# Attention followed by a two-layer MLP: one moe item moved in two units, one x multiply moved ahead of two norms, 14 more dummy matmuls

## The chip, the cores and the metric

The kernel runs on one core of one Trainium2 chip. The core has five engines that each work through their own queue in the order written: TensorE (PE, matmuls; PEld is its weight load), VectorE (DVE), ScalarE (ACT), GpSimd (POOL) and SyncE (SP, which here only issues DMAs). They meet through semaphores. The metric is the device time of one execution in microseconds (us). The profile is of one execution; its span, 415.2 us, runs from the first to the last instruction.

## The reference

```python
def rmsnorm(x, g):
    rms = np.sqrt(np.mean(x * x, axis=-1, keepdims=True) + 1e-06)
    return x / rms * g
q_n, k_n = rmsnorm(q, g_q), rmsnorm(k, g_k)        # (8, 12, 448, 64)
scores = np.matmul(q_n, k_n.transpose(0, 1, 3, 2)) / np.sqrt(64)
scores = scores - np.max(scores, axis=-1, keepdims=True)
attn = np.exp(scores)
attn = attn / (np.sum(attn, axis=-1, keepdims=True) + 1e-09)
x = np.matmul(attn, v)                             # heads side by side: (3584, 768)
h = x @ w_in                                       # w_in (768, 2048)
out = np.maximum(0.01 * h, h) @ w_out              # w_out (2048, 768)
```

## The kernel before, in words

Attention is cut into 24 units; unit u holds four heads of one batch, so three units make a batch, whose 448 positions then go through the MLP (called moe in the code). A unit has these stages, each a small function:

- Preparation, some units ahead: `load` fetches q and k, `load_v` v; `prep_sq`/`prep_sqp` square them (ACT or GpSimd), `prep_ssq` (L159, DVE) sums the squares, `prep_rinv` (L164, L165, ACT) makes the inverse root, `prep_norm` (L171, DVE) writes the normed q and k in fp16 as `n`. They are then transposed to `qkT`: on TensorE for the first units (L179 in `prep_tr`, with copies L753 and L755 on DVE), from unit 6 on by a DMA (`prep_trd`, L183), after which DVE multiplies the q part by the weights g (`prep_g`, L155).
- Scores: seven tiles of 64 keys for the four heads, in four steps d of one, two, two and two tiles (`STEPS`). `qk` (L199, TensorE) writes a tile into one of two score slots `sT` in PSUM; `ex` (L218, ACT) reads it, writes the exponential to `et` and thereby frees the slot.
- The shift inside the exponential: the maximum of the first tile (`shift_max`, L236, L238 on DVE, which makes `dg`), spread by a small matmul (`shift_mm`, L254 or L248) and read back as the bias `eb` (L255 or L249, L257).
- Sums and values: sums of `et` by matmuls with ones (L280, or L307 in `zcol`), `add_e` adds some tiles on DVE first (L292); the product with v is L367. The inverse of the sums is taken on ACT (L353, L354 in the first units; L327, L332 later, and then four DMAs, L337, spread it over the partitions as `rz`). The x multiply joins the two: `xmul` (L376), or L347 on DVE (`xmul_sb`) or on GpSimd (`xmul_pool`). It writes `xt`, the MLP's input.

The MLP of a batch is cut into items in a `queue`. A first-layer item (`moe1`, L389) is six matmuls of 128 x 448, over the six blocks of 128 inputs, into one PSUM bank `hps`, and an ACT prelu (L383) to `gt`. A second-layer item (L430) is eight matmuls of 128 x 384. The last two of the six matmuls of `moe1` read the part of `xt` that the third unit of the batch wrote.

All of the order is written by hand (`tc.manual_schedule`). The first three units are written out line by line; from unit 3 on a loop goes over units and steps. In step d it issues the scores, the exponentials and, in step 0, the sums, values and shift of the unit before. Then it gathers `jobs` (preparation of later units, x multiplies, weight differences L446 for the second layer) and calls `fill`, which takes items from the queue and issues one job after each item, and the rest of the jobs behind the last. How many items a step takes came from `fill` itself: it shared the cost of what is queued over the steps that are left before the next batch's items arrive, by the weights `WD`.

PSUM banks outside the score slots come from four buffers called `aux`, given out in turn; who gets a buffer waits until its last user is done. `warm` (L769) issues dummy matmuls of 128 x 128 whose result nobody reads; they keep TensorE busy in gaps. In the part of unit 2 the aux buffers are taken in this order: `pb` of unit 2 (shift), two for the value product of unit 1, one for the transposed q of unit 3, one for the transposed k of unit 3.

Of the kernel before, what the change touches and what calls it, by code (L numbers as in the profile page):

```python
# [18 lines left out]
def kernel(  # L19
# [18 lines left out]
    NU = B * NQ  # L38
# [73 lines left out]
    st = {}  # L112
# [62 lines left out]
    def prep_tr(u, ti, copies):  # L175
        tp = aux([P, NS, P], FP16, "tp")
        for (lo, hi), copy in copies:
            for x in range(lo, hi):
                nc.tensor.transpose(tp[:, x, :], buf(u, "n16")[:, ti, x].rearrange("p a d -> p (a d)"), ident16)  # L179
            copy(buf(u, "qkT")[:, ti, lo:hi], tp[:, lo:hi], ti == 0)  # L180
# [21 lines left out]
    def qk(u, steps):  # L202
        st[u]["sT"] = []
        for t in steps:
            sT = slot()
            score(u, t, (sT[:, 0], sT[:, 1]))
            st[u]["sT"].append((t, sT))

    def ex(u):
        s = st[u]  # L210
        if "et" not in s:
            s["et"] = epool.tile([P, NS, 2, S], FP16, tag="et", name="et")
        for t, sT in s["sT"]:
            if isinstance(sT, list):
                for a in range(2):
                    nc.scalar.activation(s["et"][:, t, a], sT[a][:, 0:S], AF.Exp, bias=s["eb"], scale=1.0)
            else:
                nc.scalar.activation(s["et"][:, t], sT[:, :, 0:S], AF.Exp, bias=s["eb"], scale=1.0)  # L218
# [6 lines left out]
    def shift_max(u):  # L225
        s = st[u]
        sT = s["sT"][0][1]
        if isinstance(sT, list):
            pm2 = small.tile([P, 2], FP32, tag="pm2", name="pm2")
            for a in range(2):  # L230
                nc.vector.tensor_reduce(pm2[:, a:a + 1], sT[a][:, 0:S], axis=AXL.X, op=ALU.max)
            s["spare"] = sT[0]
            nc.vector.tensor_reduce(s["spare"][:, 511:512], pm2, axis=AXL.X, op=ALU.max)
        else:
            s["spare"] = sT[:, 0]
            nc.vector.tensor_reduce(s["spare"][:, 511:512], sT[:, :, 0:S], axis=AXL.XY, op=ALU.max)  # L236
        s["dg"] = small.tile([P, P], FP16, tag="dg", name="dg")
        nc.vector.tensor_tensor(s["dg"], ident16, s["spare"][:, 511:512].broadcast_to([P, P]), op=ALU.mult)  # L238
# [131 lines left out]
    def xmul(u, rs=BOTH):  # L370
        s = st[u]
        b, g = divmod(u, NQ)
        if b not in xts:
            xts[b] = xpool.tile([P, NQ, 2, S], FP16, tag="xt", name="xt")
        for r in rs:
            nc.vector.tensor_tensor(xts[b][:, g, r], s["pv"][r][:, 0:S], s["rz"][:, r], op=ALU.mult)  # L376
            drop(s["pv"][r])
# [37 lines left out]
    def flush():  # L415
        while pend:
            pend.pop(0)()
# [247 lines left out]
    queue = []  # L665
# [50 lines left out]
            items += [(1.31, fn) for fn in std]  # L716
        queue.extend(items)

    WD = (3.6, 2.9, 2.8, 2.8)
    STEPS = ((0,), (1, 2), (3, 4), (5, 6))  # L720
    debt = [0.0]

    def narrow(u):
        return 4 <= u < NU - 1
# [1 line left out]
    def fed(u, d):  # L726
        return u % NQ == 0 and d == 3

    def fill(u, d, jobs):
        total = sum(c for c, _ in queue)  # L730
        left = WD[d] + 3.0
        uu, dd = u, d
        while True:
            dd += 1
            if dd == 4:
                uu, dd = uu + 1, 0
            if uu == NU or (fed(uu, dd) and (u > 3 or uu > 3)):
                break
            left += WD[dd]
        debt[0] += total * WD[d] / left  # L740
        while queue and debt[0] >= queue[0][0] * 0.5:
            c, fn = queue.pop(0)
            fn()
            debt[0] -= c
            if jobs:
                jobs.pop(0)()
        flush()
        for job in jobs:
            job()
# [17 lines left out]
    def warm(n, bank):  # L767
        for x in range(n):
            nc.tensor.matmul(bank[:, P:2 * P], onesp, onesp, start=True, stop=True)  # L769

    with tc.manual_schedule():
# [57 lines left out]
        def trn(u, ti, copy):  # L829
            prep_tr(u, ti, ((ALL, copy),))  # L830
# [91 lines left out]
        load_v(5)  # L922
        qk(2, (2,))
        ex(2)
        warm(6, st[2]["pb"])
        qk(2, (3,))
        ex(2)
        trn(3, 0, vcopy)
        trn(3, 1, vcopy)
        xmul(1)  # L930
        prep_ssq(4)
# [30 lines left out]
        for u in range(3, NU):  # L962
            for d in range(4):
                if d > 0 or u > 3:
                    qk(u, STEPS[d])
                    if d == 0:
                        shift_max(u)
                        if u == 6:
                            xmul_sb(u - 2)
                        if narrow(u - 1):  # L970
                            pv_slot(u - 1)
                            zcol(u - 1)
                            shift_mm(u)
                            pv_out(u - 1)
                        else:
                            zsum_slot(u - 1)
                            pv(u - 1)
                            shift_mm(u)
                            zinv(u - 1)
                    ex(u)  # L980
                    if d == 0 and narrow(u - 1):
                        zcol_ln(u - 1)
                if d == 2 and ADDED.get(u, 0) > 3 and u < NU - 1:
                    add_e(u)
                    if u > 4:
                        xmul_sb(u - 1)
                jobs = []

                def job(fn, *args):
                    jobs.append(lambda: fn(*args))  # L990

                if d == 0:
                    if u == 3:
                        prep_norm(4)
                        gate(4)
                    elif narrow(u - 1):
                        if u < NU - 1:
                            job(zcol_inv, u - 1)
                    else:
                        xmul(u - 1)  # L1000
                    if u + 4 < NU:
                        job(load, u + 4)
                    if u + 3 < NU:
                        load_v(u + 3)
                    if u < 6:
                        prep_sqp(u + 3)
                if d == 1 and narrow(u - 1) and not 5 <= u < 8 and ADDED.get(u, 0) < 4:
                    xmul_pool(u - 1)
                if u == NU - 1:
                    if d == 1:  # L1010
                        job(zcol_inv, u - 1)
                if fed(u, d) and u > 3:
                    push(u // NQ - 1)
                if (u, d) in ((3, 1), (4, 0)):
                    for ti in range(2):
                        prep_tr(u + 1, ti, VV)
                if d == 1 and 5 <= u < NU - 1:
                    job(prep_g, u + 1)
                if u + 2 < NU:
                    if d == 1:  # L1020
                        if ADDED.get(u) == 3:
                            job(lambda u: (prep_ssq(u + 2), add_e(u)), u)
                        else:
                            for ti in range(2):
                                job(prep_ssq, u + 2, ALL, (ti,))
                    if d == 2:
                        job(prep_rinv, u + 2)
                        for ti in range(2):
                            job(prep_norm, u + 2, ALL, (ti,))
                        if u > 3:  # L1030
                            job(prep_trd, u + 2)
                if d == 1 and 4 <= u < 8:
                    job(weight_sum, u - 4, 0)
                if d == 0 and 5 <= u < 9:
                    job(weight_sum, u - 5, 1)
                if d == 2 and u == 6:
                    job(xmul_sb, u - 1)
                if d == 1 and u == NU - 2:
                    jobs.append(lambda: None)
                    job(add_e, u)  # L1040
                if u == NU - 2 and d == 0:
                    for n, tile_ in ((1, (raws, "rq", 3)), (2, (raws, "rk", 3)), (3, None), (4, (prep_p, "sq", 3))):
                        job(win_sum, n, 1, tile_)
                    for n in (3, 1, 2, 4):
                        job(x_sum, LATE, n)
                if u == NU - 1 and d == 3:
                    job(add_e, u)
                    job(xmul_sb, u - 1)
                if d == 3 and 6 <= u < NU - 3:
                    for ti in range(2):  # L1050
                        job(prep_sq, u + 3, ALL, (ti,))
                fill(u, d, jobs)
# [4 lines left out]
        for i, ns in enumerate(((3, 1), (2, 4))):  # L1057
            c, fn = queue[i]
# [33 lines left out]
```

## Time and profile before

The median of three runs is 417.51 us (416.79 to 417.85).

| Stretch (us) | What | PE busy | DVE busy | ACT busy | PE clock | DMA share |
|---|---|---|---|---|---|---|
| 26.0 to 34.0 | end of unit 1, start of unit 2 | 6.35 of 8.0 | 6.88 | 7.32 | 1.00 | 1.10 |
| 34.0 to 42.4 | unit 2 | 7.35 of 8.4 | 7.56 | 7.37 | 1.00 | 1.12 |
| 42.4 to 57.7 | unit 3 | 14.41 of 15.3 | 12.78 | 13.46 | 1.00 | 1.15 |
| 57.7 to 70.8 | unit 4 | 12.55 of 13.1 | 11.67 | 10.19 | 1.00 | 0.95 |
| 70.8 to 84.5 | unit 5 | 13.60 of 13.7 | 12.25 | 7.68 | 1.00 | 0.99 |
| 84.5 to 97.8 | unit 6 | 13.08 of 13.3 | 11.41 | 10.01 | 1.00 | 1.00 |
| 97.8 to 112.0 | unit 7 | 14.20 of 14.2 | 12.48 | 12.99 | 1.00 | 0.66 |

A stretch is cut at the start of a unit's first exponential, roughly; busy times are unions of the engine's instructions inside it. The clock is the share that TensorE was granted. The DMA share is the time that packets took over the time of 16 engines; it can pass 1 because a packet that starts inside a stretch is counted whole. In the timeline, "[0.37 <-ACT et L218]" behind an instruction says how long its engine was idle before it, and which instruction ended that.

### The profile page before, as it was taken

The numbers are of one execution on the slowest core, as the hardware profiler recorded it, in microseconds if no ns is written. First come the engines' busy times: TensorE is split into PE (matmuls) and PEld (weight loads), VectorE is DVE, ScalarE is ACT, GpSimd is POOL, SyncE is SP. The second block draws the span as 40 slices with busy tenths as digits, with TensorE's granted clock in tenths as the row PEclk, the third lists the DMA queues.
The fourth block names the chain that finished last, engine by engine and source line by source line (L and its number), as shares of the span: only waits on it lengthen the run. The fifth ranks groups of instructions, "written<-read, shape, count | busy, mean of one in ns | idle before, by whom it ended". The sixth has DMA issues, their size and how long they took to land.

```text
span 415.2 us, 9343 instructions
## 1 busy us (share of the span) xinstructions
PE 399.3 (96%) x3817; PEld 219.1 (53%) x3817; DVE 307.7 (74%) x492; ACT 300.7 (72%) x470; POOL 68.4 (16%) x70
## 2 busy tenths in 40 slices
PE   8688999999999999999999999999999999999995
PEld 7444444554445544554445544454445557558863
DVE  5888898898788757867669757767669788557762
ACT  5898887677987699867987679867986657653600
POOL 1868432200020200010020200020001202000000
PEclk9999999999999999999999999999999999999999
DMA  6999999999565986678664896678552460032023
GB/s 207 259 255 253 240 249 141 229 174 207 138 154 92 224 213 125 150 173 182 155 155 72 220 196 136 170 147 185 158 103 47 120 160 8 10 75 77 2 55 98
DMA packets 71950, 62.41 MB, mean 150 GB/s; under 512 B 36324, under 2 KB 67044, under 8 KB 71908
## 3 DMA queue, kind: packets, MB, share of 16 engines
q1 hardware_dynamic: 61312, 49.62, 47.3%
q0 software_dynamic: 10272, 11.80, 18.3%
q8 instruction: 30, 0.49, 0.5%
q10 hardware_dynamic: 324, 0.39, 0.3%
q14 instruction: 12, 0.10, 0.1%
HBM read 45.61 MB, written 11.01 MB: 136 GB/s over the span
## 4 chain that ended last, share of the span: by engine, by line
PE 82%; DVE 9%; ACT 6%; issue 2%; DVEq 0%
PE hps L389 27%; PE sT L199 8%; PE sT L367 5%; PE ma L471 5%; PE op L430 5%; PE md L471 5%; PE bank L591 4%; PE mc L471 4%; PE bank L471 4%; ACT et L218 3%; PE mb L471 3%; PE zc L307 2%; DVE n L171 2%; PE warm L769 2%; PE sT L471 2%
## 5 line engine op out<-in xcount | busy, mean ns | idle before, releaser
L218 ACT ACTIVATE et<-sT,eb 128x896 f16<-128x896 f32 x166 | 159.4, 1008 | 26.7 <-PE sT L199 17.4
L389 PE MATMUL hps<-xt,win 128*128 128x448 f16 x600 | 121.0, 353 | 0.3 <-DVE xt L376 0.2
L389 PEld LDWEIGHTS <-win 128*128 128x128 f16 x612 | 56.8, 98 | 58.4 <-issue 10.0
L383 ACT ACTIVATE gt<-hps 128x448 f16<-128x448 f32 x100 | 53.9, 554 | 7.4 <-PE hps L389 6.4
L199 PE MATMUL sT<-qkT 64*64 64x448 f16 x664 | 52.5, 363 | 4.2 <-ACT et L218 2.8
L159 DVE TENSOR_REDUCE ssq<-sq 128x14 f32<-128x896 f32 (+2 forms) x49 | 50.1, 1059 | 0.6 <-ACT sq L148 0.6
L471 PEld LDWEIGHTS <-sa 128*128 128x128 f16 x352 | 32.8, 98 | 26.3 <-issue 6.1
L128 POOL DMA_DIRECT2D vt<-in_v_dram x24 | 17.9, 746 | 172.0 <-PE sT L367 165.2
L471 PEld LDWEIGHTS <-gt 128*128 128x128 f16 x264 | 25.2, 98 | 19.3 <-issue 2.8
L199 PEld LDWEIGHTS <-qkT 64*64 64x64 f16 x672 | 15.4, 104 | 37.3 <-issue 32.6
L322 ACT COPY x<-sT 128x896 f32<-128x896 f32 x16 | 14.5, 906 | 26.0 <-DVE sT L249 26.0
L347 POOL TENSOR_TENSOR xt<-x,rz 128x896 f16<-128x896 f32 x9 | 18.9, 2097 | 80.3 <-DMA rz<-zs 80.3
L171 DVE TENSOR_TENSOR n<-rq,rinv 128x896 f16<-128x896 f32 (+2 forms) x25 | 27.0, 1084 | 5.0 <-ACT rinv L165 5.0
L292 DVE TENSOR_TENSOR ea<-ea,et 128x896 f16<-128x896 f16 x27 | 16.9, 625 | 16.7 <-ACT et L218 15.7
L367 PE MATMUL sT<-et,vt 64*64 64x448 f16 x532 | 28.5, 349 | 0.3
L430 PE MATMUL op<-wout,gt 128*128 128x384 f16 x160 | 28.4, 326 | 0.0
L236 DVE TENSOR_REDUCE sT<-sT 128x1 f32<-128x896 f32 x22 | 24.1, 1094 | 3.6 <-PE sT L199 3.5
L367 PEld LDWEIGHTS <-vt 64*64 64x64 f16 x672 | 20.5, 107 | 11.3 <-issue 1.4
L171 DVE TENSOR_TENSOR n<-rk,rinv 128x896 f16<-128x896 f32 (+2 forms) x26 | 26.1, 1012 | 0.0
L430 PEld LDWEIGHTS <-gt 128*128 128x128 f16 x192 | 17.6, 98 | 14.4 <-issue 3.1
L471 PE MATMUL ma<-wout,gt 128*128 128x384 f16 x128 | 23.5, 326 | 0.0
L292 DVE TENSOR_TENSOR ea<-et 128x896 f16<-128x896 f16 x14 | 9.4, 673 | 11.8 <-ACT et L218 11.7
(144 smaller groups left out, 549.0 us busy)
## 6 DMA issues: line engine op xcount, KB each, us to landing
rq<-in_q_dram SPq DMA_DIRECT2D x24, 448.0 KB, 4.0
rk<-in_k_dram SPq DMA_DIRECT2D x24, 448.0 KB, 5.5
out_dram<-ost SPq DMA_DIRECT2D x52, 192.0 KB, 3.1
rz<-zs SPq DMA_DIRECT2D x76, 112.0 KB, 2.3
vt<-in_v_dram POOLq DMA_DIRECT2D x24, 224.0 KB, 4.8
win<-in_moe_w_in_dram POOLq DMA_DIRECT2D x8, 384.0 KB, 15.8
wout<-in_moe_w_out_dram POOLq DMA_DIRECT2D x2, 1536.0 KB, 28.9
out_dram<-ost SPq DMA_DIRECT2D x4, 96.0 KB, 2.1
```

The costliest lines, as they stand in the source:

```text
L159: nc.vector.tensor_reduce(buf(u, "ssq")[:, ti, :, c[0]:c[1]], buf(u, f"sq{ti}")[:, :, c[0]:c[1]], axis=AXL.X, op=ALU.add)
L171: nc.vector.tensor_tensor(buf(u, "n16")[:, ti, c[0]:c[1]].rearrange("p s a d -> p a s d"), src[:, :, c[0]:c[1]], buf(u, "rinv")[:, ti, :, ...
L199: nc.tensor.matmul(banks[a][64 * r:64 * r + 64, 0:S].rearrange("p (t x) -> p t x", t=NS), kT(u, r, a, t), qT(u, r, a), start=True, stop=True)
L218: nc.scalar.activation(s["et"][:, t], sT[:, :, 0:S], AF.Exp, bias=s["eb"], scale=1.0)
L236: nc.vector.tensor_reduce(s["spare"][:, 511:512], sT[:, :, 0:S], axis=AXL.XY, op=ALU.max)
L292: nc.vector.tensor_tensor(s["ea"], s["et"][:, 0] if t == 1 else s["ea"], s["et"][:, t], op=ALU.add)
L347: eng.tensor_tensor(xts[b][:, g], s["x32"], s["rz"], op=ALU.mult)
L367: nc.tensor.matmul(s["pv"][r][64 * a:64 * a + 64, 0:S], vts[u % NV][64 * r:64 * r + 64, a, t], s["et"][64 * r:64 * r + 64, t, a], start=(t ...
L383: nc.scalar.activation(dst, src, AF.Prelu, bias=0.0, scale=1.0, alpha=0.01)
L389: nc.tensor.matmul(hps[:, 0:S], win16[:, kt // 2, kt % 2, ts(ft, P)], xt[:, kt // 2, kt % 2], start=(kt == 0), stop=(kt == KT - 1))
L430: nc.tensor.matmul(op2[:, 0:HC], gt[:, ft, ds(col(t), P)], wout16[:, ft, ds(HC * half, HC)], start=(ft == 0), stop=(ft == FT - 1))
L471: nc.tensor.matmul(bank[:, 0:HC], a[:, f], b[:, f], start=(first and f == 0), stop=(f == HF - 1), skip_group_check=not first)
```

## The change

It has three parts.

- The number of items that each step takes is now a table, `PLAN`, a digit for each step of units 3 to 23, in place of the sharing in `fill`. For units 5 to 23 its digits are those that `fill` worked out before. In unit 3 they go from 2212 to 2122 and in unit 4 from 2212 to 1222. So in unit 3 one first-layer item moves from step 1 to step 2; in unit 4 an item moves from step 0 to step 1 and one from step 1 to step 2. The aim is to spread the items evenly between the score steps. (The division of jobs among items moves a little with it: in these two units ACT's prelus change places with exponentials and with the inverse root; DVE's order stays.)
- In step 2 of unit 6 the x multiply of unit 5 (`xmul_sb`, L347) is issued ahead of the two norms of unit 8 (L171) instead of behind them and behind the DMA transpose that follows. It is meant to reach the moe item of step 3 sooner, which reads its result.
- In the hand-written part of unit 2, 6 more dummy matmuls stand between score tiles 2 and 3, and 8 new ones between the transposes of q and k of unit 3. They fill gaps of TensorE and write to the bank `pb` of unit 2.

No work of the reference is added or left out.

```diff
-    WD = (3.6, 2.9, 2.8, 2.8)
+    PLAN = ("2122", "1222", "2112", "2122", "3232", "3322", "2322",
+            "2322", "3231", "3222", "3323", "3232", "2321", "3322",
+            "3231", "3222", "3323", "3232", "2322", "4356", "5232")
...
     def fill(u, d, jobs):
-        total = sum(c for c, _ in queue)
-        left = WD[d] + 3.0
...
-        debt[0] += total * WD[d] / left
-        while queue and debt[0] >= queue[0][0] * 0.5:
-            c, fn = queue.pop(0)
+        for n in range(int(PLAN[u - 3][d])):
+            fn = queue.pop(0)[1]
             fn()
-            debt[0] -= c
             if jobs:
                 jobs.pop(0)()
...
         qk(2, (2,))
         ex(2)
-        warm(6, st[2]["pb"])
+        warm(12, st[2]["pb"])
         qk(2, (3,))
         ex(2)
         trn(3, 0, vcopy)
+        warm(8, st[2]["pb"])
         trn(3, 1, vcopy)
...
                     if d == 2:
                         job(prep_rinv, u + 2)
+                        if u == 6:
+                            job(xmul_sb, u - 1)
                         for ti in range(2):
                             job(prep_norm, u + 2, ALL, (ti,))
...
-                if d == 2 and u == 6:
-                    job(xmul_sb, u - 1)
```

More of the change, by code (lines that the diff above doesn't have):

```diff
@@ L717, in push @@
         queue.extend(items)
-    WD = (3.6, 2.9, 2.8, 2.8)
+    PLAN = ("2122", "1222", "2112", "2122", "3232", "3322", "2322",
+            "2322", "3231", "3222", "3323", "3232", "2321", "3322",
+            "3231", "3222", "3323", "3232", "2322", "4356", "5232")
     STEPS = ((0,), (1, 2), (3, 4), (5, 6))
-    debt = [0.0]
     def narrow(u):
@@ L729, in fill @@
     def fill(u, d, jobs):
-        total = sum(c for c, _ in queue)
-        left = WD[d] + 3.0
[L732 to L739, printed above, removed]
-        debt[0] += total * WD[d] / left
-        while queue and debt[0] >= queue[0][0] * 0.5:
-            c, fn = queue.pop(0)
+        for n in range(int(PLAN[u - 3][d])):
+            fn = queue.pop(0)[1]
             fn()
-            debt[0] -= c
             if jobs:
```

## The prediction

> **What bounds the kernel now.** I read the page's shares and slices first, then the chain, then the timeline of the stretches that the diff touches, and last the waits of TensorE.
>
> ```profile
> PE 399.3 (96%) x3817; PEld 219.1 (53%) x3817; DVE 307.7 (74%) x492; ACT 300.7 (72%) x470; POOL 68.4 (16%) x70
> ...
> PEclk9999999999999999999999999999999999999999
> ...
> PE 82%; DVE 9%; ACT 6%; issue 2%; DVEq 0%
> ```
>
> TensorE (PE) is busy for 96% of the span and holds 82% of the chain, at a full clock in every slice. Its instructions run in the order written, so a stall taken out of its queue should shorten the run by that stall, unless another engine was late anyway. After 100 us the list of waits shows nothing that TensorE itself waits for beyond "issue"; from 26 to 110 us it waits 1.6 us for ACT's exponentials (four times) and some tenths elsewhere. So the edits are priced stall by stall, in four places.
>
> Unit 4 (columns: start, length, engine, line, operation, names, shapes, count, idle before it and what ended it):
>
> ```profile
> 59.66 0.54 ACT L383 ACTIVATE gt<-hps 128x448 f16<-128x448 f32 x1 [0.89 <-PE hps L389]
> ...
> 60.80 0.54 ACT L383 ACTIVATE gt<-hps 128x448 f16<-128x448 f32 x1 [0.59 <-PE hps L389]
> ...
> 64.11 1.90 ACT L218 ACTIVATE et<-sT,eb 128x896 f16<-128x896 f32 x2
> ...
> 65.31 0.38 PE L199 MATMUL sT<-qkT 64*64 64x448 f16 x4
> ...
> 66.06 0.38 PE L199 MATMUL sT<-qkT 64*64 64x448 f16 x4 [0.37 <-ACT et L218]
> ```
>
> Step 3 needs two score slots; the second comes free only when ACT has read tile 4 (until 66.01), so TensorE stands still. ACT was late because it had itself waited 0.89 and 0.59 us for moe items. Unit 3 has the same picture (a second score tile at 51.99 behind an exponential), but there VectorE (DVE) has no gap:
>
> ```profile
> 53.49 1.09 DVE L171 TENSOR_TENSOR n<-rq,rinv 128x896 f16<-128x896 f32 x1
> 54.49 1.08 DVE L171 TENSOR_TENSOR n<-rk,rinv 128x896 f16<-128x896 f32 x1
> ...
> 55.49 1.09 DVE L236 TENSOR_REDUCE sT<-sT 128x1 f32<-128x896 f32 x1
> ...
> 56.62 0.29 DVE L238 TENSOR_TENSOR dg<-ident,sT 128x128 f16<-128x128 f16 x1
> 56.96 0.10 PEld L254 LDWEIGHTS <-onesp 128*128 128x128 f16 x1 [0.44 <-DVE dg L238]
> ```
>
> The weight load of the shift matmul L254 waits for DVE's dg. Unit 6 and the x multiply:
>
> ```profile
> 91.21 2.09 DVE n L171 x2
> 93.30 1.01 DVE xt L347
> 94.31 0.04 issue
> 94.36 0.54 PE hps L389 x2
> ```
>
> This is the chain itself: two norms, then the x multiply, then the two moe matmuls that read it.
>
> **What the Trainium skill says.** "TensorE: Matmul & The Clock Gate", section "What's actually happening": the array's clock halves after an idle window of about 3.4 us. The trace agrees as far as it can: no TensorE gap near that length between 26 and 112 us, and clock 1.00 in each stretch there, so dummy matmuls have no throttle to lift. "Perfetto Trace Analysis", section "Tensor Engine Instruction (MATMUL, LD_WEIGHTS)": a matmul's shown end is an estimate, its semaphore follows the write's acknowledgement, and DVE and ACT are strict first-in-first-out. The trace fits: L179 starts 0.06 us after the DVE instruction that releases it has ended. "SBUF — State Buffer", section "Who interferes with whom": a DVE instruction with two SBUF inputs can be blocked by a GpSimd one that reads SBUF. Here the first add (L292) of unit 3 beside GpSimd's square takes 1.33 us, the later ones 0.62. Nothing in the change moves these squares.
>
> **The change, part by part.**
>
> (a) *14 warm matmuls.* One costs 0.056 us of issue (six span 0.51 us, the last 0.22 of it its own length). Six more after the six at 32.74: issue would end at 33.42 instead of 33.08, and the next score tile starts at 33.64 because it waits for ACT's L353 (ends 33.59). Hidden by that wait: cost 0. The other eight stand between the q and the k transposes of unit 3, 34.37 to 34.82, where TensorE waits until 34.97 for DVE's norm of k (ends 34.91). By issue alone they fit. But they write the bank pb, and with four "aux" banks in turn (pb, two for pv, the q transposes, then the k transposes) the k transposes take over just that bank and wait for TensorE's own last write to it. The last warm matmul begins at 34.76 and ends at 34.98; with the 0.06 us that a release takes, the k transposes start at about 35.03, not 34.97. Behind them DVE goes on without a break: copy L755 (35.57), x multiplies, squares' sums. So +0.06 us on the path; bounds 0 and 14 x 0.056 = 0.78. Gain: none, the clock is full already.
>
> (b) *One moe item later in unit 3 (2212 to 2122) and in unit 4 (2212 to 1222).* No work is added; 12 items per two units as before. Unit 4 first. From the first moe matmul (58.31) to the first score tile of unit 5 (68.75) TensorE takes 10.44 us. Work in it: seven items of 1.15 (the chain has 2.29 for 12 matmuls) = 8.03, three score steps of 0.50 = 1.50, and 0.09 lost at each of four changes from moe to scores (58.31 + 2.29 = 60.60, start 60.69) = 0.36. Sum 9.89; the rest, 0.55, is the stall. Does the new order remove it? Scores 1 and 2 come at 59.55, scores 3 and 4 at 62.34, and the third pair at 65.31 as now. ACT (a pair of exponentials takes 1.78 to the next start, a prelu 0.43 to 0.55): prelu at 59.66, pair 60.1 to 61.9, two moe prelus to 63.0, the pair of 3 and 4 to about 64.9. That is before 65.50, when TensorE asks for the second slot. ACT's later pair then ends near 68.1 (68.70 before), in time for the slot that unit 4's value product takes at about 68.4. DVE's norms wait for rinv, which comes earlier too. So -0.55; bounds 0 (ACT late after all) and -0.55 here.
>
> Unit 3 by the same sum would give back 0.57 (score tile at 51.99 instead of 51.42). I count none of it: DVE is busy without a break from the copy L753 at 46.94, which the move doesn't touch, to dg at 56.91, and L254 waits for that. TensorE merely waits longer there. Bounds 0 and -0.57.
>
> (c) *x multiply of unit 5 ahead of the two norms of unit 8.* It needs the broadcast rz: the last of the four transfers, issued at 88.40, takes 2.3, so lands at 90.7. It can start at 91.21 in place of the first norm and end at 92.30. The moe item that reads it starts at 93.31; its last two matmuls then start at 93.31 + 4 x 0.189 = 94.07 instead of 94.36: -0.29 us, and scores and value product behind them shift along. What it delays: the norms end at 94.39 instead of 93.30, so the DMA transpose of unit 8 is issued 1.09 us later. It took 6.37 us (93.36 to 99.74), and DVE's scaling L155 of that tile starts at 99.79, only 0.05 after. So L155 newly waits about 1.05 us, with sums, weight difference and adds (L159, L446, L292) queued behind it. Those meet an idle 0.92 us before the third add (105.28, waiting for an exponential) and 0.17 before the norm at 107.07; together 1.09, and TensorE takes nothing from DVE in that stretch: its prelus and exponentials are ACT's. So cost 0; bounds 0 and +1.05. The copy L434 behind the norms keeps its place, and L236 after it waits 0.56 for TensorE.
>
> Sum: 0.06 - 0.55 - 0.29 = -0.78 us, 417.51 to 416.7. TensorE is the bound from there to the end, so the gain should be kept.
>
> **Rivals.** *Unit 3 pays as well* (if the shown ends hide slack in DVE's queue): 0.06 - 1.12 - 0.29 = -1.35, 416.2. For it: the stall is as plain as unit 4's. Against: DVE's unbroken row. *Nothing is kept*: unit 5 or 6 waits for something that doesn't move, such as the transposes by DMA, with DMA at 0.95 to 1.15 of its engines until 98 us; 417.5. For it: that load, and 9% of the chain on DVE. Against: the waits found there are for engines. *Slower*: L155's wait reaches rinv, norms and the transpose of unit 9, and the score move gives nothing: 417.51 + 0.06 + 1.05 - 0.29 = 418.3; with all 14 warm matmuls on the path, 419.1. For it: 0.05 us of room at L155. Against: 1.09 us of idle DVE right behind it.
>
> **How the numbers follow.** Forecast 0.48, unit 3 too 0.30, nothing kept 0.15, slower 0.07. The forecast is 416.7. The time before has runs from 416.79 to 417.85, so a median can lie some 0.5 off: from 416.2 - 0.6 to 417.5 + 0.4, that is 415.6 to 417.9. Faster by over 0.3% is below 416.26: about a quarter of the forecast's share, seven tenths of unit 3's: 0.36. Slower is above 418.76: part of the last case and some scatter, 0.06. The rest, 0.58, lies between.
>
> **What would show it.** (a) The k transposes of unit 3 near 35.03, clock still full. (b) No wait at the sixth tile of either unit; L254 of unit 4 still at about 57.0; unit 5's first scores at about 68.2. (c) The moe matmuls of unit 6 without a gap, L155 of unit 7 waiting for a DMA. It is wrong if L254 moves forward, if unit 5's scores don't, or if the lead at 98 us (expected 0.8) has gone by the end.

## The result, and the profile after

The changed kernel takes 415.78 us (median of 4 runs, 415.42 to 416.33) against 417.3 us (4 runs, 416.79 to 417.85). The ratio is 0.9964, 95% interval 0.9947 to 0.9982; timed again with more runs (below) it is 0.9973, 0.9964 to 0.9981. So it is faster by about 0.3%, 1.1 to 1.5 us, where the prediction had 0.8 us. The time lies in the predicted range (415.6 to 417.9 us), near its lower end.

The page of the changed kernel, in the same lines as before:

```profile
PE 399.6 (96%) x3831; PEld 219.8 (53%) x3831; DVE 306.2 (74%) x492; ACT 300.7 (73%) x470; POOL 68.7 (17%) x70
...
PEclk9999999999999999999999999999999999999999
...
PE 85%; DVE 7%; ACT 6%; issue 1%; DVEq 0%
```

TensorE has its 14 matmuls more and no less work; its share of the chain rose by three points and DVE's fell by two. That is what taking waits out of TensorE's queue looks like. The diff moved the line numbers: 758 is now `warm`, 742 and 744 are the copies that were 753 and 755.

This execution ran 0.28 us late from its first units on, before anything that was changed, so places are best compared from unit 0's bias `eb` (12.29 us before, 12.57 after). In unit 4 (timeline; start, length, engine, line):

```profile
60.00 0.55 ACT L383 ACTIVATE gt<-hps 128x448 f16<-128x448 f32 x1 [0.89 <-PE hps L389]
60.44 1.90 ACT L218 ACTIVATE et<-sT,eb 128x896 f16<-128x896 f32 x2
...
63.31 1.90 ACT L218 ACTIVATE et<-sT,eb 128x896 f16<-128x896 f32 x2
...
65.65 0.57 PE L199 MATMUL sT<-qkT 64*64 64x448 f16 x8
```

ACT's second wait, 0.59 us before, is gone: the exponentials start straight after the first prelu. So the third pair of score tiles is one group of eight matmuls with no idle time, where before the second tile stood 0.37 us behind an exponential. At the end of unit 3:

```profile
56.95 0.29 DVE L238 TENSOR_TENSOR dg<-ident,sT 128x128 f16<-128x128 f16 x1
57.30 0.10 PEld L254 LDWEIGHTS <-onesp 128*128 128x128 f16 x1 [1.00 <-DVE dg L238]
```

The stall in unit 3's scores is gone too, but L254's weight load now waits 1.00 us for DVE instead of 0.44. The wait was moved, not removed. The chain through unit 6:

```profile
93.25 1.14 PE hps L389 x6
94.38 0.31 PE sT L199 x4
```

Six moe matmuls in one piece; norms and x multiply have left the chain.

### The profile page after: what moved, and what is told of

It is laid out like the page before. It is cut to its first block, busy times and chain, and to the rows that moved or that the text cites. A ratio compares the mean times of both kernels' runs of the same rounds, so it can differ in the third digit from the quotient of the medians.

```text
span 414.1 us, 9371 instructions
## 1 busy us (share of the span) xinstructions
PE 399.6 (96%) x3831; PEld 219.8 (53%) x3831; DVE 306.2 (74%) x492; ACT 300.7 (73%) x470; POOL 68.7 (17%) x70
## 4 chain that ended last, share of the span: by engine, by line
PE 85%; DVE 7%; ACT 6%; issue 1%; DVEq 0%
PE hps L389 27%; PE sT L199 9%; PE op L430 6%; PE sT L367 5%; PE ma L471 5%; PE md L471 5%; PE mc L471 5%; PE bank L591 5%; PE bank L471 4%; ACT et L218 3%; PE mb L471 3%; PE zc L307 2%; PE warm L758 2%; PE sT L471 2%; DVE n L171 1%
## 5 line engine op out<-in xcount | busy, mean ns | idle before, releaser
L347 POOL TENSOR_TENSOR xt<-x,rz 128x896 f16<-128x896 f32 x9 | 19.0, 2112 | 78.7 <-DMA rz<-zs 71.2
L171 DVE TENSOR_TENSOR n<-rq,rinv 128x896 f16<-128x896 f32 (+2 forms) x25 | 26.2, 1051 | 4.9 <-ACT rinv L165 4.9
L171 DVE TENSOR_TENSOR n<-rk,rinv 128x896 f16<-128x896 f32 (+2 forms) x26 | 26.1, 1012 | 0.0
```

Of the source, the lines that this page charges most:

```text
L171: nc.vector.tensor_tensor(buf(u, "n16")[:, ti, c[0]:c[1]].rearrange("p s a d -> p a s d"), src[:, :, c[0]:c[1]], buf(u, "rinv")[:, ti, :, ...
```

## The experiments

Each kernel was profiled and timed. The table gives, from the traces, when each unit's bias `eb` was made, counted from unit 2's `eb` and compared with the kernel before's first profile (us; minus is earlier). Counting from unit 2 leaves out an event of the clock in units 0 and 1 that is told below. "4 tiles added" means that DVE makes one add less in unit 3 (tiles of exponentials are added up before their sums are taken).

| Kernel | unit 3 | 4 | 5 | 7 | 12 | 13 | 23 | ratio to before (95%) |
|---|---|---|---|---|---|---|---|---|
| after | +0.06 | +0.06 | -0.50 | -0.79 | -0.79 | -1.09 | -1.32 | 0.9964 (0.9947 to 0.9982) |
| before again | 0.00 | +0.01 | +0.01 | +0.01 | +0.01 | -0.21 | -0.44 | 0.9995 (0.9983 to 1.0007) |
| after again | +0.05 | +0.05 | -0.51 | -0.79 | -0.79 | -1.09 | -1.32 | 0.9973 (0.9964 to 0.9981) |
| after, no dummies | 0.00 | +0.01 | -0.55 | -0.84 | -0.84 | -0.65 | -0.70 | 0.9984 (0.9976 to 0.9992) |
| dummies only | +0.05 | +0.06 | +0.06 | +0.06 | +0.06 | -0.24 | -0.48 | 0.9994 (0.9983 to 1.0005) |
| unit 3 only | 0.00 | 0.00 | 0.00 | +0.01 | +0.01 | +0.06 | -0.08 | 0.9997 (0.9984 to 1.0010) |
| unit 4 only | 0.00 | +0.01 | -0.55 | -0.55 | -0.55 | -0.52 | -0.65 | 0.9987 (0.9977 to 0.9997) |
| x multiply only | 0.00 | 0.00 | +0.01 | -0.28 | -0.27 | -0.57 | -0.81 | 0.9991 (0.9976 to 1.0007) |
| after, 4 tiles added | +0.05 | -0.40 | -0.90 | -1.19 | -1.19 | -1.48 | -1.72 | 0.9966 (0.9954 to 0.9978) |
| after, 24 dummies | +0.73 | +0.73 | +0.17 | -0.12 | +0.66 | +0.36 | +0.35 | 1.0013 (1.0005 to 1.0022) |
| before, 4 tiles added | 0.00 | +0.11 | +0.18 | +0.18 | +0.17 | -0.12 | -0.36 | 1.0005 (0.9997 to 1.0014) |
| after, dummies early | 0.00 | +0.01 | -0.55 | -0.84 | -0.49 | -0.79 | -1.03 | 0.9990 (0.9981 to 0.9998) |
| after, 4 tiles, no dummies | +0.01 | -0.45 | -0.95 | -1.24 | -1.17 | -1.47 | -1.71 | 0.9965 (0.9955 to 0.9976) |

**Before again** (no edit).

> The kernel before, unchanged, timed against itself. It prices the two places in which the profile after gained more than was predicted: 0.30 us at 187 us and 0.25 us at 319 us, where DVE's norm and DVE's s3 were blocked beside GpSimd's x multiply in the first profile (1.92 and 1.99 us instead of 1.09 and 1.30). Theory 1, chance: the blocks come from one rz transfer that landed late in that execution; a second profile has other blocks or none, and single runs differ by 0.3 to 0.6 us. Theory 2, built in: both blocks stand again at the same instructions within 0.1 us. Ratio 1.000 in either case.

Measured: ratio 0.9995. The block of DVE's norm at unit 12 stands there again (1.70 us), smaller; the second one is nearly gone (1.43 us in place of 1.99) and costs nothing. So neither theory as written: the place is built in, the size varies.

**After again** (no edit).

> The changed kernel, unchanged. Sum theory (each of the four parts as predicted, the rest chance): ratio 0.9981, and measured on the trace from unit 0's bias eb: 0.05 later at unit 3, 0.06 at unit 4, 0.51 earlier at unit 5, 0.79 earlier at unit 7, and no more than 0.3 away from 0.79 at unit 23. Theory 2 (the shift itself takes the two later blocks away): 0.79 at unit 7 and about 1.3 at unit 23 again, ratio 0.9965.

Measured: the same places to within 0.01 us as in its first profile, both later gains included, -1.32 at unit 23; ratio 0.9973, nearer to 0.9965 than 0.9981. The second theory fits: the later gains belong to the changed kernel. But they can't come from the shift, as the next two runs show.

**After, without the 14 dummies.**

```diff
-        warm(12, st[2]["pb"])
+        warm(6, st[2]["pb"])
...
-        warm(8, st[2]["pb"])
```

> The changed kernel without the 14 added dummy matmuls. If the only effect of these is the wait of the k transposes for their own bank, the eb of unit 3 comes 0.05 us earlier than with them (42.24 minus 12.29 = 29.95 from unit 0's eb, as before the change) and everything behind it keeps its order: 0.84 earlier at unit 7. Rival: they keep the clock up; then without them matmuls in units 2 to 4 show a pitch above 0.19 us or the granted clock falls below 1, and the gain shrinks by some tenths.

Measured: the predicted -0.84 at unit 7 and no loss of clock from unit 2 on. The eb of unit 3 is where it was before the change. But at unit 13 there is a loss of 0.19 instead of a gain of 0.30, though this kernel is shifted as much as the changed one. Ratio 0.9984.

**The 14 dummies only.**

```diff
-        warm(6, st[2]["pb"])
+        warm(12, st[2]["pb"])
...
+        warm(8, st[2]["pb"])
         trn(3, 1, vcopy)
```

> The kernel before with only the 14 dummy matmuls added. Own-bank theory: 0.05 us later at unit 3 and the same 0.05 at unit 7, ratio 1.0001. Hidden theory: 0.00. Rival (they pay by the clock): earlier by 0.2 us or more somewhere.

Measured: 0.05 to 0.06 later up to unit 12, as expected, and then the two gains of 0.30 and 0.24, with nothing else changed. So it is the dummies that take the later blocks away, some 145 us after they ran. The time alone does not show it (ratio 0.9994, its interval holds 1).

What links them? The profile before, at unit 12 (timeline), and after:

```profile
183.79 2.07 POOL L347 TENSOR_TENSOR xt<-x,rz 128x896 f16<-128x896 f32 x1 [8.66 <-DMA rz<-zs]
...
184.90 1.92 DVE L171 TENSOR_TENSOR n<-rq,rinv 128x896 f16<-128x896 f32 x1 [0.31 <-ACT rinv L165]
185.73 1.47 PE L471 MATMUL mc<-wout,sa 128*128 128x384 f16 x8
186.74 0.55 DVE L478 TENSOR_TENSOR ost<-md,ost 128x384 f32<-128x384 f32 x1
...
187.34 1.46 PE L471 MATMUL md<-tw,gt 128*128 128x384 f16 x8
```

```profile
182.09 2.08 POOL L347 TENSOR_TENSOR xt<-x,rz 128x896 f16<-128x896 f32 x1 [7.46 <-ACT ost L498]
...
184.39 1.09 DVE L171 TENSOR_TENSOR n<-rq,rinv 128x896 f16<-128x896 f32 x1 [0.32 <-ACT rinv L165]
185.22 1.47 PE L471 MATMUL mc<-wout,sa 128*128 128x384 f16 x8
185.40 0.55 DVE L478 TENSOR_TENSOR ost<-md,ost 128x384 f32<-128x384 f32 x1
...
186.53 1.46 PE L471 MATMUL md<-tw,gt 128*128 128x384 f16 x8
```

Before, GpSimd's x multiply started late and DVE's norm, begun beside it, took 1.92 us instead of 1.09. The add behind it came late, and TensorE waited for that add before it could write to the bank md again: its md matmuls begin 1.61 us after the mc ones, not 1.31. GpSimd was late because the last of the four rz transfers landed 3.9 us after its issue instead of 2.3. In that time a DMA queue moved one packet of 16 KB of instructions. The DMA answers for 180.5 to 181.5 us before, and for 177 to 178 us after (queue and kind: packets, MB, their time as a share of 16 engines):

```profile
q8 instruction: 1, 0.02, 9.3%
```

```profile
q8 instruction: 1, 0.02, 6.7%
```

A rival is the other traffic: two stores of results (L409) are issued 0.7 and 1.3 us behind that rz transfer. But they stand at the same place after the change, without a packet of instructions, and there the transfer lands in 2.3 us. The same answers for the data queue, 180.5 to 181.5 us before and 180.4 to 181.4 us after:

```profile
q1 hardware_dynamic: 213, 0.18, 80.6%
```

```profile
q1 hardware_dynamic: 221, 0.18, 83.4%
```

There are 30 such fetches in a run. The Trainium skill ("Perfetto Trace Analysis", section "The 4-stage abstract model") has instructions at 64 bytes; TensorE's 7634 rows make 29.8 packets of 16 KB, so this queue is, by that estimate, TensorE's instructions. More TensorE instructions in unit 2 make every later fetch come earlier. All fourteen profiles sort by when the fetch comes, counted from the issue of the last rz transfer of a unit (the loss is against the shortest way from unit 12 to 13 in the fourteen):

| Profiles | fetch, unit 12 (us) | x multiply starts after that issue (us) | lost by unit 13 (us) |
|---|---|---|---|
| before, before again, no dummies, unit 3 only, unit 4 only, x multiply only | 1.20 to 1.27 | 3.67 to 4.24 | 0.30, 0.08, 0.48, 0.35, 0.33, 0.00 |
| the other eight | -1.53 to -3.89 | 2.46 to 2.49 | 0.00 |

The losses differ because the packet takes 1.08 to 1.60 us. In each of the six the transfer lands 1.21 to 1.24 us after the packet's end. A multiply that starts up to 3.67 us after the issue costs nothing; at 3.84, 4.07 and 4.24 us the loss is 0.08, 0.30 and 0.48 us, so what comes later is lost one for one.

The second gain, in unit 20, comes by another way. In the kernel before, the fetch there (306.5 us) begins between the issues of the four rz transfers. The second issue then takes SyncE 1.40 us instead of 0.59, GpSimd's multiply starts 0.8 us later, and DVE's L458 beside it is blocked. Before and after:

```profile
311.74 1.99 DVE L458 TENSOR_TENSOR sa<-gt 128x512 f16<-128x512 f16 x1
```

```profile
310.93 1.30 DVE L458 TENSOR_TENSOR sa<-gt 128x512 f16<-128x512 f16 x1
```

In eight profiles a fetch falls there; one issue takes 0.85 to 1.40 us, and four of them lose 0.10 to 0.24 us, the other four 0.01 at most. In the other six each issue takes 0.60 us or less and nothing is lost.

**Unit 3's item only.**

```diff
-    WD = (3.6, 2.9, 2.8, 2.8)
+    PLAN = ("2122", "2212", "2112", "2122", "3232", "3322", "2322",
```

> The kernel before with only unit 3's item moved (2122). VectorE-bound theory: the sixth score tile of unit 3 comes 0.55 us earlier (no wait for an exponential), but L254 of unit 4 and unit 4's eb stay where they were (45.28 us after unit 0's eb), so 0.00 at unit 7, ratio 1.0000. Rival (unit 3 pays): unit 4's eb is 0.3 to 0.57 earlier.

Measured: the sixth score tile 0.54 us earlier, L254 0.02 us later, unit 4's eb 0.00. In its timeline L254's weight load waits 1.01 us for DVE's dg. The rival (unit 3 pays) falls.

**Unit 4's items only.**

```diff
+    PLAN = ("2212", "1222", "2112", "2122", "3232", "3322", "2322",
```

> The kernel before with only unit 4's items moved (1222). Unit 5's eb 0.55 us earlier, kept to unit 23: ratio 0.9987. If unit 4 needed unit 3's move for it (rival), less than 0.3.

Measured: -0.55 at unit 5 and still -0.55 at unit 12; ratio 0.9987. It does not need unit 3's move.

**The x multiply only.**

```diff
+                        if u == 6:
+                            job(xmul_sb, u - 1)
                         for ti in range(2):
...
-                if d == 2 and u == 6:
-                    job(xmul_sb, u - 1)
```

> The kernel before with only the x multiply ahead of the norms of unit 8. The moe matmuls of unit 6 lose their gap: unit 7's eb 0.29 us earlier; DVE's scaling L155 of unit 7 waits up to 1.05 us for the DMA transpose, and unit 8's eb still is 0.29 earlier because DVE's gaps behind it take the wait up. Rival: the wait goes through, unit 8 or 9's eb falls back by 0.1 us or more. Ratio 0.9993 against 1.000.

Measured: -0.28 at unit 7, kept. But the wait of L155 isn't there at all (its timeline in unit 7):

```profile
100.03 0.95 DVE L446 TENSOR_TENSOR tw<-wout 128x1536 f16<-128x1536 f16 x1
100.89 0.45 DVE L155 TENSOR_SCALAR qkT<-qkT,gcol 128x896 f16<-128x896 f16 x1
```

It follows the weight difference without a gap. The transpose was issued later but landed 4.99 us after its issue (95.75 to 100.74), not 6.37; in the changed kernel 4.53 us (94.14 to 98.67).

**One add less on DVE in unit 3.**

```diff
-    ADDED.update({3: 5, 4: 5, NU - 1: 5})
+    ADDED.update({3: 4, 4: 5, NU - 1: 5})
```

> The changed kernel with one add of exponential tiles less on DVE in unit 3 (0.73 us off DVE) and four more matmuls of 0.19 us in pairs (0.19 us on TensorE) in their place. If DVE is what holds L254 of unit 4, unit 4's eb comes 0.35 to 0.45 earlier than in the changed kernel (DVE's dg 0.73 earlier, TensorE ready about 0.4 before it was). If DVE is not the holder: no gain or 0.19 later.

Measured: unit 4's eb 0.45 us earlier than in the changed kernel; L254's weight load waits 0.36 us, no longer 1.00. DVE was the holder.

**24 dummies in place of 8 ahead of the k transposes.**

```diff
-        warm(8, st[2]["pb"])
+        warm(24, st[2]["pb"])
```

> The changed kernel with 24 instead of 8 dummy matmuls ahead of the k transposes. The 16 more cost 16 x 0.056 = 0.90 us of issue and stand behind the 0.05 us of the eight, in the path through DVE. Own-bank theory: unit 3's eb 0.90 later than in the changed kernel, that is 30.91 us after unit 0's, and all of it kept at unit 7 (0.11 later than before in place of 0.79 earlier). If dummy matmuls there were hidden: less than 0.5 later.

Measured: 0.67 later than in the changed kernel, between the two expectations. 24 x 0.056 = 1.34, less 0.60 us from the end of the q transposes' issue (34.37) to the start of the k transposes (34.97) before: 0.74, and 0.73 was found at unit 3. The k transposes start as soon as the last dummy is issued (36.24 to 36.30): in this program they wait for DVE's semaphore alone, while in the changed kernel they wait for one of TensorE's own as well, and start 0.06 us after the last dummy's shown end. Why the two programs differ in this is not shown. This kernel has 60 TensorE instructions more than before; a fetch now falls 1.27 us after the last rz issue of unit 9, GpSimd's multiply starts 4.43 us after it, a norm takes 2.41 us and unit 10's eb is 0.79 us late. In unit 18 it happens again (fetch at 1.34, multiply at 3.97, 0.22 us lost). The pattern moved to other units.

**The kernel before with one add less in unit 3** (the `ADDED` edit above, on the kernel before).

> The kernel before with one add less on DVE in unit 3 and four more matmuls in pairs, and the old places of the moe items. If the gain of 0.45 us at unit 4 needs both (TensorE's stall at the sixth tile gone, and DVE relieved), this kernel gains nothing at unit 4: between 0.05 earlier and 0.19 later than before. If the add alone was the limit: 0.3 us or more earlier at unit 4, with the stall of 0.5 us still there.

Measured: unit 4's eb 0.11 later, 0.18 at unit 5, with the stall at the sixth tile still there (0.37 us). So the item's move in unit 3 and the relief of DVE are worth nothing alone and 0.45 us together.

**21 dummies early, in unit 0, in place of the 14.**

```diff
-        warm(8, wb)
+        warm(14, wb)
         qk(0, (3,))
         ex(0)
+        warm(5, wb)
...
         qk(0, (4,))
         ex(0)
+        warm(10, wb)
```

> The changed kernel without its 14 dummy matmuls; in their place 21 others in gaps between 14 and 17.3 us (unit 0: 6 more ahead of score tile 3, 5 behind it, 10 behind tile 4), where five of ten profiles so far fall to half clock at 16.7 to 18.1 us and lose 0.96 to 1.43 us by unit 1's eb. If that fall follows from too little TensorE work in the window before it, the profile has full clock from 7 us to the end, unit 1's eb is within 0.1 us of its place in the undisturbed profiles (8.28 us after unit 0's), single runs scatter less, and the median is about 0.5 us under the changed kernel's: ratio 0.9965 to 0.997. If the fall has another cause, the profile may still show it and the ratio is 0.998.

(Four of the profiles until then had the fall, not five.) Before again, over two stretches; columns: stretch, length, busy time of PE, PEld, DVE, ACT and POOL, granted clock, DMA share, GB/s:

```profile
17.90:21.30 3.40, 3.40 (x31) 1.92 (x30) 2.08 (x5) 1.44 (x3) 3.40 (x5) 0.50 1.16 258
21.30:24.70 3.40, 3.19 (x64) 2.17 (x65) 2.46 (x5) 3.27 (x7) 1.91 (x4) 1.00 1.07 240
```

Measured: with the early dummies full clock from 7 to 412 us and unit 1's eb in its place, but ratio 0.9990, no better than without any added dummies (0.9984; the intervals overlap). The median did not fall below the changed kernel's, and the 13 runs still spread over 1.5 us. Its 42 more instructions put a fetch 1.29 us behind unit 9's last rz issue, which cost 0.35 us at unit 10. One profile without the fall does not show that the dummies prevented it: nine of the other thirteen had none either, and one of the 13 timed runs with early dummies had a mean granted clock of 0.994 (of the kernel before, timed beside it, six of 41 had 0.996 or less). All changes of the clock in these traces lie a whole number of steps of 3.41 us apart. In the step ahead of the four falls TensorE was busy for 41, 50, 60 and 60% of the time (by the shown ends); in the other ten profiles no step up to 40 us is under 62%, and with the early dummies none under 71%. That speaks for too little work in a step. But near the end of three runs a step of 42 or 50% was followed by one of full clock, so the busy share alone does not decide it. The cause stays open.

**The version that the runs point to**: one add less in unit 3, no added dummies.

> The version that the runs point to: the changed kernel with one add less on DVE in unit 3 and without the 14 dummy matmuls. If the parts add up: unit 4's eb 0.45 us earlier than before (0.39 with the dummies, 0.06 for leaving them out), unit 5's 0.95, unit 7's and all to unit 12's 1.24 us earlier, apart from a fall of the clock in units 0 and 1, if there is one; ratio 0.997, against 0.9966 for the version with the dummies and 0.9973 for the changed kernel. If the dummies do pay somewhere after all, its ratio is above that of the version with them by more than their intervals.

Measured: -0.45, -0.95 and -1.24 at units 4, 5 and 7 as summed; at unit 12 it stands at -1.17. Ratio 0.9965. It can't be told from the version with dummies (0.9966); both lie below the changed kernel's 0.9973, with intervals that overlap. Its own fetch falls before the last of unit 12's transfers (-1.53 us; the matmuls in place of the add are 8 more TensorE instructions), so it has that gain without added dummies.

## Why the prediction came out as it did

**(a) The 14 dummies.** Cost: predicted +0.06, measured +0.05 to +0.06, twice, and with the mechanism named: the last dummy's shown end is 35.26, the k transposes start at 35.31. "Gain: none, the clock is full already" is the step that failed. The clock was full from unit 2 to 412 us in all profiles, as argued, so the reason was right and the conclusion wrong: 28 more instructions in TensorE's queue moved its fetches off the rz transfers of unit 12, and off those near 306 us. Over the six profiles with the old place of the fetch, the loss by unit 13 averages 0.26 us, and at unit 21 another 0.11 (0.24, 0.01, 0.19, 0.10, 0.11, 0.01). This term belongs in the sum at about -0.37, but as an average: single profiles lose from 0.01 to 0.67 us. That it falls out as a gain is luck. Dummies aren't needed for it (the kernel before with 4 tiles added has no added ones, 8 TensorE instructions more, and both gains), and 16 more of them bring new losses of 0.79 and 0.22 us.

The prediction could have seen the stall. It read from the list of waits that TensorE waits for nothing after 100 us. But the gap shown ahead of the late md matmuls is 0.14 us, because a matmul's shown end is an estimate, and that is too small to be listed; the delay shows only in the 1.61 us from one group to the next. It also named the collision of GpSimd with a DVE instruction of two inputs, but looked for it at the squares alone, not at the x multiply.

**(b) The moe items.** Unit 4: predicted -0.55, measured -0.56 in the changed kernel and -0.55 alone. Unit 3: predicted 0, measured 0.00 alone. The rival that counted it (-1.35 us) gave a time near the measured one, for a reason that did not hold. Two slips in the working carry no weight: the two units hold 14 items, not 12 (the sum rightly counts seven in one), and seven times 1.15 is 8.05.

**(c) The x multiply.** Predicted -0.29, measured -0.28 to -0.29 in the changed kernel and alone. The 1.05 us wait of L155 did not come. The step took over the transpose's landing time, 6.37 us. That does not stay the same: in the six profiles without this edit the transpose lands 5.9 to 6.4 us after its issue, in the eight with it 4.5 to 5.6. It could be the loads of q and k (issued at 90.40 and 91.04, landing until 96.51), but in the kernel with 24 dummies the k load ends 3.2 us after the transpose's issue, as before the change, and the transpose lands in 4.70 us; so the reason is open. Only in the changed kernel with 4 tiles added does L155 wait for it, 0.39 us, and unit 8's eb loses nothing by that. The step gave it cost 0, so the sum is not touched.

**The sum.** Predicted -0.78, at units 7 to 12 measured -0.79. With the missing -0.37 it is -1.16 us, ratio 0.9972, against 0.9973 measured in the longer timing. Agreement that close is chance: that interval (0.9964 to 0.9981) spans 0.7 us and reaches the ratio of the predicted sum. On the trace, though, the missing part is plain: both profiles of the changed kernel end at -1.32. So the time of 416.7 was too high by the term that (a) left out. The claim that a lead at 98 us is kept to the end held for the changed kernel, both times, and the stretch from unit 23's eb to the end takes 60.5 us in all profiles. It isn't a rule: where a fetch falls badly, 0.35 us (early dummies) or 0.79 us (24 dummies) are lost again. Of the rivals, "nothing is kept" and "slower" found no support. The fetch as the cause of the late transfer rests on fourteen profiles that sort without an exception, on landings that follow the packet's end, and on adding and removing the dummies; no run moved the fetch by other means than TensorE's own instructions.

## What to carry to other kernels

Price a reordering stall by stall, and ask of each stall which engine's row has no gap up to the point where the two meet: of two equal stalls here one was worth 0.55 us and the other nothing until DVE had 0.73 us less to do. A change in the number of instructions was not only that here: it moved every later instruction fetch, which cost or saved up to 0.8 us, 100 to 145 us later. So differences of a few tenths of a per cent should be placed on the trace before they are credited to the edit.

## What the runs showed of the hardware

- One 16 KB instruction packet, taking 1.08 to 1.60 us, delayed a transfer issued 1.20 to 1.27 us before it from 2.3 us to 3.5 to 4.1 us. In three cases where the packet began 1.95 to 2.02 us after the issue the transfer landed in 2.3 to 2.4 us. Through GpSimd's multiply and DVE's norm (1.09 us alone, up to 2.41 beside it) it reached TensorE.
- In four of fourteen profiles the granted clock was 0.50 for 3.41 or 6.83 us from 16.7 to 18.1 us on, where TensorE is busy with many short gaps and has no idle time over 0.9 us. Unit 1's eb came 0.96 to 1.43 us later. That is about as large as the scatter of either kernel's four runs in the first timing (0.9 to 1.1 us), and comes before anything that the change touches. Of the 53 runs of the kernel before that were timed beside "before again", the 13 with a mean granted clock of 0.996 or less took 417.95 us on average, the other 40 416.89. The idle window of about 3.4 us that the prediction speaks of was not there.
- A wait of TensorE for its own last write to a bank cost 0.056 us after that write's shown end.
